# A linear-attention and MLP kernel on one core: the rows of a head's last part interleaved, one transfer for three, issued by ScalarE

## The chip, the cores and the metric

The kernel runs on one core of one Trainium2 chip. The metric is the device time in microseconds (us) of one execution. Three executions of the kernel before took 394.83, 394.56 and 392.82 us: a median of 394.56 us.

## What is computed

```
r, k, v, w: [4, 8, 768, 48] (batch, heads, sequence, head_dim), u: [8, 48]
state = 0                                  # [B, H, 48, 48]
for t in range(768):
    kt, vt, rt, wt = k[:, :, t], v[:, :, t], r[:, :, t], w[:, :, t]
    y[:, :, t] = rt @ (state + outer(u * kt, vt))
    state = wt[..., None] * state + outer(kt, vt)
x = y.transpose(0, 2, 1, 3).reshape(3072, 384)      # 8 heads of 48 side by side
h = max(x @ w1, x @ w2, x @ w3)                     # [3072, 768]
out = h @ w_out                                     # [3072, 384]
```

All arrays are float32.

## The kernel before, in words

The sequence is cut into chunks of 128 tokens. A unit is one chunk of one batch: 24 units (`NK`), numbered chunk by chunk. For each unit attention scales r and k by running products of the decay (VectorE scans, L397 and L412, and the product L421), makes scores on TensorE, masks them, and adds the part that comes from the carried state. ScalarE also squares the products to check that none ran out of range (L426). The result of a unit lies in a PSUM tile `y`, turned: feature by token.

Four units make one half (`HT` = 512 tokens), so there are six halves. `x` is a buffer of 128 partitions by 4 slots by 512 tokens, with two buffers in turn. ScalarE copies a unit's result from `y` to its columns of `x` (`result`, L627). Eight heads of 48 features must fill three slots of 128 rows. Each slot has one head in rows 0 to 47 and another in rows 64 to 111, which leaves rows 48 to 63 and 112 to 127 free. The two heads left over come in the fourth slot (`x[..., KT, ...]`, rows 0 to 47 and 64 to 111). Their 48 rows are spread, 16 each, over the free rows of slots 0 to 2. This is done by transfers within the on-chip memory, at L635: for each of the two heads three transfers of 16 rows, one per slot. In the first half only its last 256 columns need that; there VectorE's and ScalarE's work is densest, and the three transfers of the second head are on ScalarE's queue. In the other five halves all six are on SyncE's (SP's) queue, which also carries the loads of `tin` (L262), `kr` (L249), `v` (L252), the weights (L320) and the stores of the output (L755).

The MLP then works on `x` with products in two parts: ScalarE rounds a slot to `x_hi` (L134), VectorE makes the rest `x_lo` (L135), and TensorE multiplies both with the weights (`up`, L169), groups of nine matmuls of 512 columns; the second layer is `down`, L203. Weight rows are permuted on the host to match the rows of `x` (`row` in `_layout`).

The order of instructions on each engine is written out by hand: a string of steps (`PARTS`) for the first part, a round of steps (`ORD`) for each later unit, and a generator for the MLP. TensorE alternates between a half's MLP and later units of attention, and its order is fixed. Around a half's end the steps are: result of its fourth unit (L627), transfers (L635), the rest of the MLP of the half before, `x_hi` and `x_lo`, and the first `up` of the new half.

The kernel also has a slow path (after L807), taken if the check fails; it isn't taken here.

Of the kernel before, what the change touches and what calls it, by code (L numbers as in the profile page):

```python
# [39 lines left out]
ds = bass.ds  # L40

B, H, S, D = 4, 8, 768, 48
DM, FF = 384, 768
NP = 4
C = 128
# [9 lines left out]
HC = C // 2  # L55
VW = H * D * 3 // 2
NH = B * S // HT
KT = DM // 128
# [51 lines left out]
def kernel(ctx: ExitStack, tc, tin, nat, u_flat, u_pair, v_t, w_flat, out, ytr):  # L110
    nc = tc.nc
# [112 lines left out]
    with ExitStack() as fast:  # L224
# [391 lines left out]
        def result(k):  # L616

            half, slot = divmod(k, CPH)
            if half not in xt:
                xt[half] = x_p.tile([128, NP, HT], F32, name="x")  # L620
            x = xt[half]
            if k < SEW:
                nc.scalar.copy(out=x[:, 0:KT, slot * C:(slot + 1) * C], in_=prep[k]["y"])
                got.add(k)
                return
            to_x = x[0:112, :, slot * C:(slot + 1) * C].rearrange("p (h s) t -> p h s t", h=2)
            nc.scalar.copy(out=to_x, in_=prep[k]["y"][0:112])  # L627
            at, to = next(p for p in SUBS if p[0] <= slot < p[1]) if half == 0 else (0, CPH)
            got.add(k)
            due = all(half * CPH + i in got for i in range(at, to))  # L630
            cols = slice(at * C, to * C)
            for lo in (0, 64) if due else ():
                for j in range(KT):
                    eng = nc.scalar if lo and half == 0 else nc.sync
                    eng.dma_start(out=x[lo + 48:lo + 64, j, cols], in_=x[lo + 16 * j:lo + 16 * j + 16, KT, cols])  # L635

        steps = dict(m=midway, i=check_w, j=check_w, X=scores, M=take, T=transposes, R=from_state, U=to_state, S=state, Z=decayed, V=values, Y=values_more, E=result, n=load,
                     b=prep_scan_b, p=prep_floor, q=prep_inv, f=prep_scan_f, r=prep_rk, c=prep_check, d=prep_diag1, e=prep_diag2)
# [169 lines left out]
    with tc.If(rv != 0), ExitStack() as slow:  # L808
# [9 lines left out]
        with tc.For_i(0, B) as b:  # L818
            for pr in range(NP):
                wt = seq.tile([128, S], F32, name="wt")  # L820
                rt = seq.tile([128, S], F32, name="rt")
                kt = seq.tile([128, S], F32, name="kt")
                uk = seq.tile([128, S], F32, name="uk")
                uc = seq.tile([128, 1], F32, name="uc")
                vb = wk.tile([128, S], F32, name="vb")
                for t in (wt, rt, kt, uc):
                    nc.vector.memset(t[32:64, :], 0.0)
                for hh in range(2):
                    rows = slice(64 * hh, 64 * hh + 48)
                    for t, o in ((wt, pr * WS + 1), (rt, RK + pr * C), (kt, RK + (NP + pr) * C)):  # L830
                        for c in range(NCH):
                            nc.sync.dma_start(out=t[rows, c * C:(c + 1) * C],
                                              in_=tin[ds(b, 1), c, rows, o:o + C].rearrange("a p n -> (a p) n"))
                    nc.sync.dma_start(out=uc[rows, :], in_=u_pair[pr, hh])
                nc.vector.tensor_scalar(out=uk[0:112, :], in0=kt[0:112, :], scalar1=uc[0:112, :], scalar2=None, op0=ALU.mult)
                for j in range(KT):
                    with tc.For_i(0, 16) as i:
                        vb = wk.tile([128, S], F32, name="vb")
                        kv = wk.tile([128, S], F32, name="kv")
                        st = wk.tile([128, S + 1], F32, name="st")  # L840
                        yo = wk.tile([2, S], F32, name="yo")
                        nc.vector.memset(vb[32:64, :], 0.0)
                        for hh in range(2):
                            nc.sync.dma_start(
                                out=vb[64 * hh:64 * hh + 48, :],
                                in_=v_t[ds(b, 1), 2 * pr + hh, ds(i + 16 * j, 1), :].rearrange("a e t -> (a e) t").broadcast_to([48, S]))
                        nc.vector.memset(st[0:112, 0:1], 0.0)
                        nc.vector.tensor_tensor(out=kv[0:112, :], in0=kt[0:112, :], in1=vb[0:112, :], op=ALU.mult)
                        nc.vector.tensor_tensor_scan(out=st[0:112, 1:S + 1], data0=wt[0:112, :], data1=kv[0:112, :],
                                                     initial=0.0, op0=ALU.mult, op1=ALU.add)  # L850
                        nc.vector.tensor_tensor(out=kv[0:112, :], in0=uk[0:112, :], in1=vb[0:112, :], op=ALU.mult)
                        nc.vector.tensor_tensor(out=kv[0:112, :], in0=kv[0:112, :], in1=st[0:112, 0:S], op=ALU.add)
                        nc.vector.tensor_tensor(out=kv[0:112, :], in0=kv[0:112, :], in1=rt[0:112, :], op=ALU.mult)
                        for q in range(2):
                            z = ps_z.tile([2, S // 2], F32, name="z")
                            nc.tensor.matmul(z[:, :], lhsT=sel[0:112, :], rhs=kv[0:112, q * (S // 2):(q + 1) * (S // 2)],
                                             start=True, stop=True)
                            nc.vector.tensor_copy(out=yo[:, q * (S // 2):(q + 1) * (S // 2)], in_=z[:, :])
                        for hh in range(2):
                            slot, at = 2 * hh + pr // 2, 64 * (pr % 2)  # L860
                            if slot < KT:
                                dst = ytr[slot, ds(i + at + 16 * j, 1), ds(b, 1), :]
                            else:
                                dst = ytr[j, ds(i + at + 48, 1), ds(b, 1), :]
                            nc.sync.dma_start(out=dst.rearrange("a b t -> (a b) t"), in_=yo[hh:hh + 1, :])
# [54 lines left out]
def _layout(r, k, v, w, u, moe_w1, moe_w2, moe_w3, moe_w_out):  # L920

    def heads(a):
        return a.reshape(B, NP, 2, NCH, C, D).transpose(0, 3, 2, 5, 1, 4)

    tin = np.zeros((B, NCH, 128, TU), np.float32)
    tin[:, :, 48:64, :WC] = 1.0
    tin[:, :, :, :WC:WS] = 0.0
    for half in range(2):
        rows = tin[:, :, 64 * half:64 * half + D]
        rows[..., :NP * WS].reshape(B, NCH, D, NP, WS)[..., 1:] = heads(w)[:, :, half]  # L930
        rows[..., RK:RK + NP * C] = heads(r)[:, :, half].reshape(B, NCH, D, NP * C)
        rows[..., RK + NP * C:TU] = heads(k)[:, :, half].reshape(B, NCH, D, NP * C)
        rows[..., WC:WC + NP] = u.reshape(NP, 2, D)[:, half].T

    def natural(a):
        return a.reshape(B, H, NCH, C, D).transpose(0, 2, 3, 1, 4).reshape(B, NCH, C, H * D)

    nv, turned = natural(v), lambda a: np.roll(a[..., H * D // 2:], HC, axis=2)
    parts = [nv, turned(nv)]
    for a in (natural(k), natural(r)):  # L940
        a = np.concatenate([a[..., 0:H * D // 2], turned(a)], axis=3)
        parts.append(a.reshape(B, NCH, C, NP, 2, D).swapaxes(3, 4).reshape(B, NCH, C, H * D))
    nat = np.concatenate(parts, axis=3)
    padded = np.zeros((B, C, H, HC), np.float32)
    padded[..., 0:D] = nv[:, 0].reshape(B, C, H, D)
    late = np.roll(padded[:, :, NP:], HC, axis=1)
    bits = np.zeros((B, C, 2, KT, HC), np.float32)
    bits[..., D:HC] = late[:, :, 1::2, 0:D].reshape(B, C, 2, KT, D // KT)
    first = [padded[:, :, 0:NP].reshape(B, C, NP * HC), nv[:, 0, :, NP * D:], late[:, :, 0::2].reshape(B, C, 2 * HC), bits.reshape(B, C, DM)]
    nat[0:SEW, 0, :, 0:VW + DM] = np.concatenate(first, axis=2)[0:SEW]  # L950
    row = np.empty((KT, 128), np.int64)
    head = lambda j, par: 4 * (j % 2) + 2 * par + j // 2
    for j in range(KT):
        for par in range(2):
            row[j, 64 * par:64 * par + 48] = head(j, par) * D + np.arange(48)
            row[j, 64 * par + 48:64 * par + 64] = head(KT, par) * D + 16 * j + np.arange(16)
    ws = np.stack([moe_w1, moe_w2, moe_w3])
    w_in = ws[:, row.reshape(-1), :].reshape(3, KT, 128, FT, 128).transpose(3, 0, 2, 1, 4).reshape(3 * FT, 128, PC)
    w_all = np.concatenate([w_in, moe_w_out.reshape(FT, 128, DM)])
    if w_all.dtype == np.float64:  # L960
        w_all = np.append(w_all.reshape(-1), np.zeros(1)).view(np.int64)
    return {
        "tin": tin, "nat": nat, "u_flat": u.reshape(NP, 2, D).swapaxes(0, 1).reshape(H * D), "u_pair": u.reshape(NP, 2, D, 1),
        "v_t": v.transpose(0, 1, 3, 2), "w_all": w_all,
    }
# [18 lines left out]
```

## Time and profile before

| | |
|---|---|
| median of three executions | 394.56 us |
| the profiled execution | 396.12 us |
| its span | 394.4 us |
| TensorE busy | 384.3 us (97%) |
| VectorE, ScalarE, GpSimd busy | 261.1, 174.4, 79.3 us |
| bytes moved | 58.44 MB, a mean of 148 GB/s |
| transfers of L635 | 33 issued by SP, 3 by ScalarE |

The span is what the profiler recorded; the 1.7 us between it and the execution's own time lie outside. TensorE's busy time comes from modelled ends of pipelined matmuls: neighbours overlap, so that a short delay of a matmul can show as busy time. Starts of instructions tell more than the sum of busy times.

### The profile page before, as it was taken

To read this page: it belongs to the slowest core of one execution; us is meant where nothing else is said; L and a number is where in the kernel's file an instruction comes from. 1 tells how busy PE (TensorE), PEld (TensorE's weight loads), DVE (VectorE), ACT (ScalarE), POOL (GpSimd) and SP (SyncE) were. 2 spreads that over 40 slices of the span, in tenths; PEclk is the share of its full clock that TensorE was granted. 3 is DMA by queue.
4 is the path that set the end of the run, shared out by engine and by line. 5 is a ranking of instruction groups with operands and counts; after the bars stand their busy time and mean duration, and the time that the engine had idled before them with its cause. 6 is when DMAs were issued, how large, how long until landed. Compare 5 with 4: busy or idle time off the path is not lost.

```text
span 394.4 us, 10610 instructions
## 1 busy us (share of the span) xinstructions
PE 384.3 (97%) x4496; PEld 319.6 (81%) x4496; DVE 261.1 (66%) x399; ACT 174.4 (44%) x378; POOL 79.3 (20%) x102
## 2 busy tenths in 40 slices
PE   8999999999999999999999999999999999999994
PEld 3678876777688889888889888889888889878893
DVE  6899899987679976485688485688476531243310
ACT  4687788644434454334433533433543333331210
POOL 3000000131343252143134143134223100000000
PEclk9999999999999999999999999999999999999999
DMA  8992796403713431474342774342962113300011
GB/s 285 403 336 88 262 401 235 149 2 112 224 27 143 152 125 42 130 301 152 121 165 67 244 281 147 127 165 68 293 208 77 42 42 99 122 1 1 2 41 47
DMA packets 24680, 58.44 MB, mean 148 GB/s; under 512 B 3184, under 2 KB 6736, under 8 KB 24624
## 3 DMA queue, kind: packets, MB, share of 16 engines
q1 hardware_dynamic: 21216, 48.59, 35.6%
q10 hardware_dynamic: 3408, 9.09, 7.4%
q8 instruction: 37, 0.61, 0.7%
q14 instruction: 19, 0.16, 0.1%
HBM read 51.87 MB, written 4.72 MB: 143 GB/s over the span
## 4 chain that ended last, share of the span: by engine, by line
PE 86%; DMA 6%; DVE 3%; ACT 2%; issue 1%; SPq 1%; ACTq 0%
PE psm L169 54%; PE psm L203 16%; PE grams L480 3%; PE y L605 3%; PE y L518 3%; PE psm L502 2%; DMA x<-in_nat_dram 2%; DMA tin<-in_tin_dram 1%; DMA u_bc<-in_u_flat_dram 1%; PE grams L533 1%; DMA w<-in_w_all_dram 1%; DMA x<-x 1%; PE grams L203 1%; PE y L203 1%; PE grams L451 1%
## 5 line engine op out<-in xcount | busy, mean ns | idle before, releaser
L169 PE MATMUL psm<-x_hi,w 128*128 128x512 f32 x576 | 184.3, 394 | 0.2 <-ACT x_hi L134 0.2
L169 PEld LDWEIGHTS psm<-x_hi,w 128*128 128x128 f32 x576 | 108.2, 188 | 23.6 <-ACT x_hi L134 0.5
L169 PE MATMUL psm<-x_lo,w 128*128 128x512 f32 x288 | 112.5, 391 | 0.2 <-DVE x_lo L135 0.2
L154 DVE TENSOR_TENSOR m<-psm,m 128x512 f32<-128x512 f32 x64 | 43.8, 687 | 45.6 <-PE psm L169 42.9
L203 PE MATMUL psm<-w,h_hi 128*128 128x384 f32 x264 | 70.1, 362 | 0.0
L169 PEld LDWEIGHTS psm<-x_lo,w 128*128 128x128 f32 x288 | 54.1, 188 | 11.6 <-DVE x_lo L135 0.7
L203 PEld LDWEIGHTS psm<-w,h_hi 128*128 128x128 f32 x264 | 47.7, 188 | 5.0
L134 ACT CAST h_hi<-m 128x512 fp32r<-128x512 f32 x32 | 19.7, 620 | 44.0 <-DVE m L154 44.0
L203 PE MATMUL psm<-w,h_lo 128*128 128x384 f32 x116 | 38.9, 335 | 0.0
L461 POOL TENSOR_SCALAR_AFFINE_SELECT a<-sums 64x512 f32<-64x512 f32 x32 | 22.5, 703 | 72.2 <-DVE sums L458 71.1
L397 DVE TENSOR_TENSOR_SCAN gf<-tin,d_bwd 112x517 f32<-112x517 f32 x24 | 30.2, 1259 | 10.2 <-DMA tin<-in_tin_dram 9.0
L406 POOL TENSOR_SCALAR d_fwd<-gf 112x4 f32<-112x4 f32 x24 | 6.6, 277 | 142.3 <-DVE gf L397 134.7
L135 DVE TENSOR_TENSOR h_lo<-m,h_hi 128x512 fp32r<-128x512 f32 x32 | 23.7, 745 | 17.0 <-ACT h_hi L134 16.9
L169 PE MATMUL psm<-x,w 128*128 128x256 f32 (+1 forms) x126 | 33.9, 418 | 0.0
L412 DVE TENSOR_TENSOR_SCAN gf<-tin,d_fwd 112x517 f32<-112x517 f32 x24 | 33.1, 1380 | 0.3
L426 ACT ACTIVATE gf<-gf 112x1034 f32<-112x1034 f32 x24 | 25.7, 1070 | 10.3 <-DVE tin L421 10.2
L421 DVE TENSOR_TENSOR tin<-tin,gf 112x1024 f32<-112x1024 f32 x24 | 30.1, 1254 | 0.0
L438 POOL TENSOR_TENSOR kr<-kr,u_bc 128x384 f32<-128x384 f32 x16 | 28.6, 1790 | 1.3
L169 PEld LDWEIGHTS psm<-x,w 128*128 128x128 f32 x126 | 23.0, 190 | 6.7 <-issue 3.6
L135 DVE TENSOR_TENSOR x_lo<-x,x_hi 128x512 fp32r<-128x512 f32 x18 | 11.4, 689 | 21.9 <-ACT x_hi L134 14.2
L207 ACT COPY m<-psm 128x384 f32<-128x384 f32 x22 | 10.5, 476 | 30.4 <-PE psm L203 30.3
L152 ACT COPY m<-psm 128x512 f32<-128x512 f32 x32 | 18.5, 581 | 9.0 <-PE psm L169 7.7
(93 smaller groups left out, 462.8 us busy)
## 6 DMA issues: line engine op xcount, KB each, us to landing
tin<-in_tin_dram SPq DMA_DIRECT2D x24, 512.0 KB, 4.5
w<-in_w_all_dram SPq DMA_DIRECT2D x25, 384.0 KB, 7.5
w<-in_w_all_dram ACTq DMA_DIRECT2D x23, 384.0 KB, 3.6
v<-in_nat_dram SPq DMA_DIRECT2D x24, 288.0 KB, 5.3
tin<-in_tin_dram SPq DMA_DIRECT2D x24, 262.5 KB, 5.2
kr<-in_nat_dram SPq DMA_DIRECT2D x16, 384.0 KB, 5.1
out_dram<-m SPq DMA_DIRECT2D x22, 192.0 KB, 2.4
x<-x SPq DMA_DIRECT2D x30, 32.0 KB, 3.0
```

Of the source, the lines that this page charges most:

```text
L134: nc.scalar.copy(out=hi, in_=src)
L135: rest = lambda: nc.vector.tensor_tensor(out=lo, in0=src, in1=hi.bitcast(F32), op=ALU.subtract)
L152: nc.scalar.copy(out=m[:, cols], in_=ps[:, cols])
L154: nc.vector.tensor_tensor(out=m[:, cols], in0=ps[:, cols], in1=m[:, cols], op=ALU.max)
L169: nc.tensor.matmul(ps[:, cols], lhsT=wt[i][:, ct * 128:(ct + 1) * 128], rhs=x[part][:, ct, cols], start=(n == 0), stop=(n == KT * len(term ...
L203: nc.tensor.matmul(pss[tt][:, 0:DM], lhsT=ht[f][:, tok], rhs=wt[FT * 3 + f][:, :], start=(f == 0 and i == 0), stop=(f == FT - 1 and i == l ...
L397: nc.vector.tensor_tensor_scan(out=g[0:112, ::-1], data0=t[0:112, 0:WC][:, ::-1], data1=d_bwd[0:112, ::-1], initial=0.0, op0=ALU.mult, op1 ...
L412: nc.vector.tensor_tensor_scan(out=prep[k]["f"][0:112, :], data0=tbuf[k % NB][0:112, 0:WC], data1=d_fwd[0:112, :], initial=0.0, op0=ALU.mu ...
L421: nc.vector.tensor_tensor(out=both[0:112], in0=both[0:112], in1=by[0:112], op=ALU.mult)
L426: nc.scalar.activation(out=flat, in_=flat, func=AF.Square, accum_out=acc[0:112, k:k + 1])
L438: nc.gpsimd.tensor_tensor(out=n[:, 0, :], in0=n[:, 0, :], in1=u_bc[:, :], op=ALU.mult)
L461: nc.gpsimd.affine_select(out=a[o:o + HC, 0:H, :], in_=cs[o:o + HC, :].unsqueeze(2).broadcast_to([HC, H, HC]), pattern=[[0, H], [1, HC]], ...
```

## The change

In the first free rows of slot j stood rows 16j to 16j + 15 of the left-over head. After the change row n of the head goes to slot n mod 3: free row p of slot j takes row 3p + j. In this form one transfer from 48 partitions to 16 partitions by 3 slots says what three said. Two transfers per half stand where six stood: in the first half one on SP and one on ScalarE, in the other five both on ScalarE. The layout of the first chunk's values, the permutation of the weight rows and the slow path follow the new order of rows.

```
             due = all(half * CPH + i in got for i in range(at, to))
             cols = slice(at * C, to * C)
             for lo in (0, 64) if due else ():
-                for j in range(KT):
-                    eng = nc.scalar if lo and half == 0 else nc.sync
-                    eng.dma_start(out=x[lo + 48:lo + 64, j, cols], in_=x[lo + 16 * j:lo + 16 * j + 16, KT, cols])
+                eng = nc.scalar if lo or half else nc.sync
+                eng.dma_start(out=x[lo + 48:lo + 64, 0:KT, cols], in_=x[lo:lo + 48, KT, cols])
...
-                                in_=v_t[ds(b, 1), 2 * pr + hh, ds(i + 16 * j, 1), :].rearrange("a e t -> (a e) t").broadcast_to([48, S]))
+                                in_=v_t[ds(b, 1), 2 * pr + hh, ds(i * KT + j, 1), :].rearrange("a e t -> (a e) t").broadcast_to([48, S]))
...
-                                dst = ytr[slot, ds(i + at + 16 * j, 1), ds(b, 1), :]
+                                dst = ytr[slot, ds(i * KT + (at + j), 1), ds(b, 1), :]
...
-    bits[..., D:HC] = late[:, :, 1::2, 0:D].reshape(B, C, 2, KT, D // KT)
+    bits[..., D:HC] = late[:, :, 1::2, 0:D].reshape(B, C, 2, D // KT, KT).swapaxes(3, 4)
...
-            row[j, 64 * par + 48:64 * par + 64] = head(KT, par) * D + 16 * j + np.arange(16)
+            row[j, 64 * par + 48:64 * par + 64] = head(KT, par) * D + j + KT * np.arange(16)
```

On ScalarE, at the end of the second half (`gf` is the decay products, `m` an output tile, `w` a weight), the order before and the order of the change:

```order
L627 COPY x<-y 112x4x128
L426 ACTIVATE gf,sums<-gf 112x1034
L207 COPY m<-psm 128x384
L134 CAST w_1436<-w_217 128x768
L400 COPY dec_144<-gf 112x4
L134 CAST x_hi<-x 128x512 x3
```

```order
L627 COPY x<-y 112x4x128
L634 DMA x<-x 16x3x512 x2
L426 ACTIVATE gf,sums<-gf 112x1034
L207 COPY m<-psm 128x384
L134 CAST w_1428<-w_217 128x768
L400 COPY dec_144<-gf 112x4
L134 CAST x_hi<-x 128x512 x3
```

Two issues now stand between the result's copy and the check; nothing else changed place. At the ends of the third to sixth halves ScalarE has the same pair at the same place.

On SP, the same stretch before and after:

```order
L262 DMA tin_108<-in_tin_dram 128x525
L262 DMA tin_108<-in_tin_dram 128x1024
L635 DMA x<-x 16x512 x6
L249 DMA kr<-in_nat_dram 128x768
L252 DMA v<-in_nat_dram 128x576
L755 DMA out_dram<-m 128x384 x2
```

```order
L262 DMA tin_108<-in_tin_dram 128x525
L262 DMA tin_108<-in_tin_dram 128x1024
L249 DMA kr<-in_nat_dram 128x768
L252 DMA v<-in_nat_dram 128x576
L754 DMA out_dram<-m 128x384 x2
```

The six issues are gone from between the load of `tin` and that of `kr`.

## Rows read from the trace of the kernel before

**Rows 1.** The page, busy time of each engine.

```profile
PE 384.3 (97%) x4496; PEld 319.6 (81%) x4496; DVE 261.1 (66%) x399; ACT 174.4 (44%) x378; POOL 79.3 (20%) x102
```

**Rows 2.** Waits of TensorE: waiter, releaser, us in total, times, longest.

```profile
PE grams L451 <- DVE scur L554: 0.7, 1, 0.7
...
PE psm L169 <- DVE x_lo L135: 0.2, 1, 0.2
PE psm L169 <- ACT x_hi L134: 0.2, 1, 0.2
```

**Rows 3.** Timeline, 92 to 108 us: start, duration, engine, line [idle before <- releaser].

```profile
93.72 2.58 SPq L262 DMA_DIRECT2D tin<-in_tin_dram  x2
...
94.80 0.58 ACT L627 COPY x<-y 112x512 f32<-112x512 f32 x1 [0.58 <-PE y L605]
...
96.39 4.68 SPq L635 DMA_DIRECT2D x<-x  x6
...
102.07 1.66 ACT L134 CAST x_hi<-x 128x512 fp32r<-128x512 f32 x3 [1.83 <-DMA x<-x]
...
102.72 1.90 DVE L135 TENSOR_TENSOR x_lo<-x,x_hi 128x512 fp32r<-128x512 f32 x3 [3.51 <-ACT x_hi L134]
```

**Rows 4.** The same timeline, TensorE alone.

```profile
102.19 0.34 PE L203 MATMUL psm<-w,h_lo 128*128 128x384 f32 x1
...
102.75 0.50 PE L169 MATMUL psm<-x_hi,w 128*128 128x512 f32 x1 [0.22 <-ACT x_hi L134]
...
103.47 0.50 PE L169 MATMUL psm<-x_lo,w 128*128 128x512 f32 x1 [0.23 <-DVE x_lo L135]
...
103.81 0.63 PE L169 MATMUL psm<-x_hi,w 128*128 128x512 f32 x2
```

**Rows 5.** TensorE's timeline at the start of the fourth half, 210 to 226 us.

```profile
222.36 0.33 PE L203 MATMUL psm<-w,h_lo 128*128 128x384 f32 x1
...
222.99 0.62 PE L169 MATMUL psm<-x_hi,w 128*128 128x512 f32 x2
```

**Rows 6.** Line L635: issue durations in ns min/median/max; landing in us min/median/max.

```profile
L635 SPq DMA_DIRECT2D x<-x x33: 512/585/1592, 38.7 to 334.7; - x33
...
L635 ACTq DMA_DIRECT2D x<-x x3: 602/612/856, 38.7 to 40.3; - x3
...
DMA to landing us min/median/max: 1.8/2.3/4.5
```

**Rows 7.** Timelines of ACT, SP and DVE, 36 to 76 us, one after another.

```profile
38.73 2.15 ACTq L635 DMA_DIRECT2D x<-x  x3
40.93 1.28 ACT L434 ACTIVATE kr<-tin 112x128 f32<-112x128 f32 x4 [2.23 <-issue]
...
38.73 1.87 SPq L635 DMA_DIRECT2D x<-x  x3
...
43.29 1.23 DVE L397 TENSOR_TENSOR_SCAN gf<-tin,d_bwd 112x517 f32<-112x517 f32 x1 [1.14 <-ACT gf L426]
```

**Rows 8.** Timelines of ACT, DVE and PE, later in that stretch.

```profile
54.30 0.37 ACT L152 COPY h_hi<-psm 128x256 f32<-128x256 f32 x1
...
54.88 0.42 DVE L154 TENSOR_TENSOR h_hi<-psm,h_hi 128x256 f32<-128x256 f32 x1
...
74.05 0.70 PE L451 MATMUL grams<-tin,kr 48*64 48x64 f32 x32 [0.69 <-DVE scur L554]
```

**Rows 9.** Timelines of ACT and PE at the start of the fifth half.

```profile
279.30 1.66 ACT L134 CAST x_hi<-x 128x512 fp32r<-128x512 f32 x3 [0.50 <-DMA x<-x]
...
280.97 0.39 PE L169 MATMUL psm<-x_hi,w 128*128 128x512 f32 x1
```

**Rows 10.** Busy time of each engine by stretch: us, PE, PEld, DVE, ACT, POOL, clock, DMA share, GB/s.

```profile
50.00:60.00 10.00, 10.00 (x109) 6.64 (x110) 9.86 (x16) 8.33 (x18) 0.22 (x1) 1.00 1.03 401
95.38:102.07 6.69, 6.69 (x27) 4.66 (x26) 1.88 (x3) 2.37 (x6) 1.32 (x2) 1.00 0.49 143
...
273.81:279.30 5.49, 5.49 (x34) 5.49 (x33) 2.53 (x4) 2.98 (x9) 1.37 (x3) 1.00 0.52 144
```

## The prediction

> **What bounds the kernel now.** I read the page first. TensorE is busy for 384.3 us of the 394.4 us span [rows 1]; its order is fixed and the change removes no matmul, so only waits of TensorE can be won. I then listed those waits. Most belong to the start of the program. Three can touch this change: 0.2 us for `x_hi` and 0.2 us for `x_lo` before L169, once each, and one of 0.7 us for VectorE's new state (L554) before L451 [rows 2]. The reader sees from this list alone that the prize is about 1 us in 394, and that there is nothing to win at the other ends of halves: `x_hi` and `x_lo` each made TensorE wait once, although six halves begin.
>
> Those times use modelled ends of matmuls, so I went to the starts in the timeline. At the start of the second half TensorE begins its last L203 at 102.19, and the third matmul on the new `x` begins at 103.81, which is 1.62 us later [rows 4]. At the start of the fourth half, where nothing is waited for, the same sequence takes 222.36 to 222.99, or 0.63 us [rows 5]. The late `x` costs 1.62 - 0.63 = 0.99 us there. Upstream the reader sees why. ScalarE has the result in `x` at 95.38 (94.80 + 0.58). SP is still busy with a load of `tin` from 93.72 and starts the first transfer at 96.39; six issues take 4.68 us, to 101.07; `x_hi` starts at 102.07 after ScalarE sat idle for 1.83 us for the transfer; and VectorE's `x_lo` at 102.72 [rows 3]. Most of the 6.7 us from result to `x_hi` is spent issuing.
>
> **Term 1: the second half.** The change takes away six issues on SP and puts two on ScalarE, right behind the copy. Three issues on ScalarE's queue have a median of 612 ns, and 33 on SP one of 585 ns [rows 6]. What an issue with three rows per destination row costs isn't in the trace. Its bounds are 0.51 us, the shortest issue of one part, and 1.84 us, three of ScalarE's (3 x 0.612). I take 0.61 us, since it is one instruction of the same kind with the same 16 destination rows. Two end at 95.4 + 1.2 = 96.6. Landing takes 1.8 to 4.5 us after an issue [rows 6]; because the load of `tin` is in flight then, I take the 4.5: 101.1. One `x_hi` cast is 0.62 us later and one `x_lo` 0.69 us after that (1.66 us for three casts, 1.90 us for three differences with their overlaps [rows 3]), so the first pair is there at about 101.7 and 102.4. TensorE without a delay wants them at 102.36 and 102.59 (a step of about 0.17 us after 102.19 and one of about 0.23 us, as 0.63 us makes three steps [rows 5]). The wait goes: -0.99 us. With the bounds of issue and landing, `x` is complete between 95.4 + 1.0 + 1.8 = 98.2 and 95.4 + 3.7 + 4.5 = 103.6. The late end is 1.5 us past today's 102.07, so this term lies between -0.99 and +1.5 us.
>
> The Trainium skill speaks against the step to another queue ("DMA: Bandwidth & Descriptors", section "Issuing engines are not separate DMA queues"): transfers from several engines share the same DMA engines, and only the sequencer's time to issue is saved, "which is usually small relative to the DMA itself". By that rule term 1 would be near 0, and the time 394.1. The trace differs at this place: six issues take 4.68 us and a landing 2.3 us in the median.
>
> **Term 2: the first half.** At 38.73 ScalarE issues three transfers in 2.15 us, and then starts L434 at 40.93 with 2.23 us of waiting put down to issuing; SP spends 1.87 us on its three. Further down ScalarE's queue VectorE waits 1.14 us for ScalarE's check (L426) before its scan at 43.29 [rows 7]. One issue in place of three frees ScalarE about 1.4 us earlier (2.15 - 0.61 = 1.5 at most), so this wait of 1.14 us goes. VectorE then shows no idle time until it releases L554, for which TensorE waits 0.69 us at 74.05 [rows 8]. How much of the 1.14 us is still there 30 us later depends on what VectorE would wait for next. The tightest place that I found is L154 at 54.88, behind ScalarE's copy that ends at 54.67 (54.30 + 0.37) [rows 8]: 0.21 us of room. That copy stands behind work that waits for weights, and SP's two issues fewer let the next weight loads go about 1.3 us earlier (1.87 - 0.6), so the room may be wider. The DMA engines are full here (share 1.03, 401 GB/s [rows 10]), and a start that much earlier shortens the backlog. The gain lies between 0 and 0.69 us; I take the middle of 0.21 and 0.69: -0.45 us.
>
> **What costs nothing.** In the second to sixth halves ScalarE gets 1.2 us of issuing behind the copy. The transfers wait for the copy's end, and behind them stand the check, an output copy (L207) and `dec`. ScalarE is busy for 2.37 of 6.69 us between copy and `x_hi` in the second half and 2.98 of 5.49 us in the fifth [rows 10], so idle times of 4.3 and 2.5 us cover it. Without that cover it would cost up to 1.2 us at an end of a half. An earlier `x` in the later halves earns nothing, since `x_hi` already starts before TensorE asks: at 279.30 for 280.97 [rows 9]. SP's 33 issues become 1, and loads of `kr` and `v` and the stores go out up to 4.7 us earlier; TensorE shows no wait for them, so 0. The permuted rows, the layout and the slow path move the same bytes: 0.
>
> **The sum** is -0.99 - 0.45 = -1.44 us. Against the profiled execution's own 396.12 us that gives 394.7, and against the median of 394.56, which I use, 393.1 us. I count 0.5% (2.0 us) as the least that a measurement can tell from no change; the three executions themselves lie 2.0 us apart.
>
> **The rivals.**
> 1. *The issues were not the delay.* `x` still lands at about 102, because the transfers wait behind the `tin` load in the DMA engines. For it: landings of up to 4.5 us [rows 6]. Against it: the first transfer would start 1 us sooner on a queue of its own, and the last issue ended only at 101.07 [rows 3]. This is also what the skill's rule above would make of it. Then only term 2 is left: 394.56 - 0.45 = 394.1 us.
> 2. *More than I count.* Term 2 comes in full (-0.69 us), and ScalarE's and VectorE's earlier start shortens some of the small delays that modelled ends hide, by 0.3 us or more: 394.56 - 0.99 - 0.69 - 0.3 = 392.6 us or less. For it: VectorE is busy for 9.86 of 10 us at 50 to 60 us [rows 10], so any time it wins may count. Against it: no row shows those hidden delays.
> 3. *ScalarE pays.* A merged issue costs three single ones, 1.84 us, or 3.7 us for a pair. In the fifth half 2.5 us of idle time cover it and 1.2 us are left; `x_hi` starts 1.67 us before TensorE needs it [rows 9], of which a cast and a difference take about 1.3 less a step of 0.23, so some 0.6 us is lost. The second half would keep at least part of its gain. From 393.1 + 0.6 to 393.1 + 1.6, with 394.2 in the middle.
> 4. *The merged transfer does not spread* over the DMA engines, and so the time gets worse. An engine moves about 401 / 16 = 25 GB/s [rows 10]; one transfer has 48 x 512 x 4 bytes = 98 KB, 3.9 us on one engine, and two in line 7.9 us. With 0.6 us of issue and 2.3 us of landing `x` is complete 10.8 us after the copy: 106.2 in the second half, with `x_hi` at 106.8, 4.4 us too late in place of 0.99. In the fifth half, whose copy ends at 273.81 (where its stretch of rows 10 begins), it is complete at 284.6, 5.3 us after today's 279.30; with 1.67 - 0.62 = 1.05 us of cover that is 4.3 us late; the fourth and sixth are alike. Together 3.4 + 3 x 4.3 - 0.45 = 15.9, or 410 us. It decides from the point where the pair lands more than about 7 us after the copy. Against it: 16 destination rows are what each single transfer had, and those landed in 2.3 us; the 48 source rows are the new thing.
>
> By the skill's rule on how many engines a transfer uses (same page, section "Why a DMA increments its semaphore by 16 and not by 1"), the largest number up to 16 that divides the outer sizes of both sides counts; 16 divides 48 and 16, so rival 4 falls. No row shows how the transfers were split.
>
> **How the numbers follow.** My forecast has a chance of 0.50, rival 1 0.14, rival 2 0.24 (with the draws of the forecast that a spread of 2 us puts beyond 0.5%), rival 3 0.08, rival 4 0.04. Faster by over 0.5% is rival 2: 0.24. Slower is rival 4: 0.04. The rest is within 0.5%: 0.72. The likeliest is 393.1 us. The range goes down past rival 2 by the 1 us that the executions lie to one side, 391.6, and up past rivals 1 and 3 to 395.2, which also holds part of term 1's bad end; rival 4 and the tails are left out.
>
> **What would show it.** Right: in the second half the transfers start at the copy's end on ScalarE's queue, about 1 us before today's place; `x_hi` waits for no transfer; third matmul on the new `x` 0.63 us after the last L203; no wait of VectorE for L426 near 42 us, and a wait of under 0.5 us before L451 near 74. Later halves show the same starts relative to their copy. Wrong: landings of the pair over 5 us, issues over 1 us, a new wait of TensorE at the start of a half, or a time that moves by over 2 us while these waits do what I say.

## The result and the profile after

The change takes 396.14 us in the median of 20 executions (393.71 to 399.97), the kernel before, timed beside it, 393.85 us (392.02 to 395.31): ratio 1.0057, 95% interval 1.0038 to 1.0076. It is slower, by 2.3 us, just over what the prediction called measurable; the forecast was 1.44 us faster, and 396.14 lies above the range. The profiled execution of the change took 399.25 us (span 397.3), that of before 396.12 (span 394.4). Both are long executions, 3.1 and 2.3 us above their medians: they show how time is lost, and the medians how much.

The page first: busy times and the granted clock of TensorE in 40 slices.

```profile
PE 385.8 (97%) x4496; PEld 320.5 (81%) x4496; DVE 259.7 (65%) x399; ACT 174.2 (44%) x378; POOL 77.5 (20%) x102
...
PEclk9999999999899999999999999999999999999999
```

TensorE is busy for 1.5 us more than in [rows 1] with the same 4496 matmuls, and one slice of its clock (99 to 109 us) reads 8. So matmuls ran slower somewhere there; that alone is not a wait. Its waits are next, in the form of [rows 2].

```profile
PE psm L169 <- ACT x_hi L134: 1.7, 1, 1.7
...
PE psm L169 <- DVE x_lo L135: 0.7, 2, 0.5
...
PE grams L451 <- DVE scur L554: 0.2, 1, 0.2
```

The wait for L554 fell from 0.7 to 0.2: the first half did what term 2 said. The two waits for `x`, which were to vanish, grew from 0.2 and 0.2 to 1.7 and 0.7. The timeline of the second half's start, to be held against [rows 3]:

```profile
93.19 1.94 SPq L262 DMA_DIRECT2D tin<-in_tin_dram  x2
...
94.26 0.58 ACT L627 COPY x<-y 112x512 f32<-112x512 f32 x1 [0.59 <-PE y L605]
...
94.88 1.25 ACTq L634 DMA_DIRECT2D x<-x  x2
...
95.17 0.42 SPq L249 DMA_DIRECT2D kr<-in_nat_dram  x1
...
95.65 0.58 SPq L252 DMA_DIRECT2D v<-in_nat_dram  x1
...
102.63 0.99 POOL L437 TENSOR_TENSOR kr<-kr 128x384 f32<-128x384 f32 x1 [5.63 <-DMA kr<-in_nat_dram]
102.96 1.66 ACT L134 CAST x_hi<-x 128x512 fp32r<-128x512 f32 x3 [3.27 <-DMA x<-x]
103.61 2.71 DVE L135 TENSOR_TENSOR x_lo<-x,x_hi 128x512 fp32r<-128x512 f32 x3 [4.96 <-ACT x_hi L134]
...
103.63 0.50 PE L169 MATMUL psm<-x_hi,w 128*128 128x512 f32 x1 [1.66 <-ACT x_hi L134]
...
105.77 0.80 PE L169 MATMUL psm<-x_lo,w 128*128 128x512 f32 x1 [0.45 <-DVE x_lo L135]
```

Up to the issue all goes as predicted: ScalarE has the result at 94.84 (94.26 + 0.58), and both transfers are issued by 96.13, where SP needed until 101.07. But `x_hi` starts 8.12 us after the result (102.96 - 94.84), before it was 6.69 (102.07 - 95.38). The loads of `kr` and `v`, which stood behind six issues on SP, leave SP at 95.17 and 95.65, so `kr` is issued ahead of the second transfer, which starts at 95.52, and `v` behind its start. The same stretch by DMA issues (KB each, median us from issue to landing), before:

```profile
kr<-in_nat_dram SPq DMA_DIRECT2D x1, 384.0 KB, 3.5
v<-in_nat_dram SPq DMA_DIRECT2D x1, 288.0 KB, 3.7
...
x<-x SPq DMA_DIRECT2D x6, 32.0 KB, 3.9
```

And after:

```profile
tin<-in_tin_dram SPq DMA_DIRECT2D x1, 512.0 KB, 6.0
...
kr<-in_nat_dram SPq DMA_DIRECT2D x1, 384.0 KB, 7.3
v<-in_nat_dram SPq DMA_DIRECT2D x1, 288.0 KB, 8.5
...
x<-x ACTq DMA_DIRECT2D x2, 96.0 KB, 6.6
```

An `x` transfer now lands after 6.6 us in the median (7.4 the later, as line L634 shows below, so 5.8 the other), `kr` after 7.3 in place of 3.5, `v` after 8.5 in place of 3.7. Issuing was cheap, as counted; line L634 over the whole program:

```profile
L634 ACTq DMA_DIRECT2D x<-x x11: 563/603/672, 38.7 to 335.3; - x11
...
DMA to landing us min/median/max: 2.3/2.9/7.4
```

What the late `x` cost in this execution can be read off. From TensorE's last L203 to the third matmul on the new `x`, 0.63 us where nothing is late [rows 5], it took 1.62 us before [rows 4] and 3.05 after (101.64 to 104.69): 1.43 us more. The next matmul on an `x_lo` then waits as well; from the third, it starts 1.08 us on, before 0.47: 0.61 us more. And then each step takes twice its time. Windows of 1 us (busy time of PE, PEld, DVE, ACT, POOL; clock, DMA share, GB/s):

```profile
100.00:101.00 1.00, 1.00 (x5) 0.61 (x4) 0.00 (x0) 0.00 (x0) 0.00 (x0) 1.00 1.11 215
...
102.00:103.00 1.00, 0.00 (x0) 0.00 (x0) 0.00 (x0) 0.04 (x1) 0.37 (x1) 1.00 0.53 180
...
104.00:105.00 1.00, 0.78 (x4) 0.49 (x3) 1.00 (x2) 0.99 (x3) 1.00 (x1) 1.00 0.00 2
105.00:106.00 1.00, 0.55 (x3) 0.23 (x2) 1.00 (x2) 0.00 (x0) 0.72 (x2) 0.75 0.12 45
106.00:107.00 1.00, 1.00 (x3) 0.81 (x4) 1.00 (x3) 0.00 (x0) 0.00 (x0) 0.50 1.14 232
107.00:108.00 1.00, 1.00 (x3) 0.79 (x3) 1.00 (x3) 0.46 (x1) 0.00 (x0) 0.50 0.82 266
...
109.00:110.00 1.00, 1.00 (x6) 0.83 (x5) 0.20 (x1) 0.00 (x0) 0.00 (x0) 1.00 0.72 277
```

The granted clock is 1.00 through the wait, 0.50 (1.2 GHz) from 106 to 108 and 1.00 again from 109. Seven matmuls took 3.15 us (105.77 to 108.92) where seven at full clock take 1.59: 1.56 us. Together 1.43 + 0.61 + 1.56 = 3.60 us. Landmarks of TensorE, taken from the chain of waits that ended last, give the same: from the first half's first L169 to the run of 33 matmuls behind L451 it took 50.71 us before and 50.22 after (-0.49); from there to the first L518 behind the second half's start 41.41 and 45.01 (+3.60); from there to the last run of L169 235.26 and 235.16.

### The profile page after: what moved, and what is told of

The parts are those of the page before. It is cut to its first block, busy times and chain, and to the rows that moved or that the text cites. A ratio compares the mean times of both kernels' runs of the same rounds, so it can differ in the third digit from the quotient of the medians.

```text
span 397.3 us, 10559 instructions
## 1 busy us (share of the span) xinstructions
PE 385.8 (97%) x4496; PEld 320.5 (81%) x4496; DVE 259.7 (65%) x399; ACT 174.2 (44%) x378; POOL 77.5 (20%) x102
## 4 chain that ended last, share of the span: by engine, by line
PE 85%; DVE 6%; DMA 5%; issue 1%; ACT 1%; SPq 0%; ACTq 0%; DVEq 0%
PE psm L169 54%; PE psm L203 16%; PE grams L480 3%; PE y L605 3%; PE y L518 3%; DMA x<-x 2%; PE psm L502 2%; DMA x<-in_nat_dram 2%; DMA tin<-in_tin_dram 1%; PE grams L533 1%; DVE cv L343 1%; DVE w L349 1%; DVE x_lo L135 1%; PE grams L203 1%; PE y L203 1%
## 5 line engine op out<-in xcount | busy, mean ns | idle before, releaser
L169 PE MATMUL psm<-x_hi,w 128*128 128x512 f32 x576 | 185.1, 396 | 1.7 <-ACT x_hi L134 1.7
L169 PEld LDWEIGHTS psm<-x_hi,w 128*128 128x128 f32 x576 | 108.8, 189 | 25.3 <-ACT x_hi L134 2.0
L169 PE MATMUL psm<-x_lo,w 128*128 128x512 f32 x288 | 113.2, 393 | 0.7 <-DVE x_lo L135 0.7
L203 PE MATMUL psm<-w,h_hi 128*128 128x384 f32 x264 | 70.0, 361 | 0.0
L169 PEld LDWEIGHTS psm<-x_lo,w 128*128 128x128 f32 x288 | 54.5, 189 | 12.4 <-DVE x_lo L135 1.4
L203 PEld LDWEIGHTS psm<-w,h_hi 128*128 128x128 f32 x264 | 47.7, 188 | 5.0
L203 PE MATMUL psm<-w,h_lo 128*128 128x384 f32 x116 | 38.9, 335 | 0.0
L169 PE MATMUL psm<-x,w 128*128 128x256 f32 (+1 forms) x126 | 33.9, 418 | 0.0
L412 DVE TENSOR_TENSOR_SCAN gf<-tin,d_fwd 112x517 f32<-112x517 f32 x24 | 32.1, 1338 | 0.3
L426 ACT ACTIVATE gf<-gf 112x1034 f32<-112x1034 f32 x24 | 25.6, 1070 | 11.5 <-DVE tin L421 10.0
L169 PEld LDWEIGHTS psm<-x,w 128*128 128x128 f32 x126 | 23.0, 190 | 6.8 <-issue 3.8
L438 POOL TENSOR_TENSOR kr<-kr,u_bc 128x384 f32<-128x384 f32 x16 | 27.4, 1716 | 1.3
L135 DVE TENSOR_TENSOR x_lo<-x,x_hi 128x512 fp32r<-128x512 f32 x18 | 12.2, 732 | 19.5 <-ACT x_hi L134 19.5
```

The lines of the kernel that those rows point to most:

```text
L135: rest = lambda: nc.vector.tensor_tensor(out=lo, in0=src, in1=hi.bitcast(F32), op=ALU.subtract)
L169: nc.tensor.matmul(ps[:, cols], lhsT=wt[i][:, ct * 128:(ct + 1) * 128], rhs=x[part][:, ct, cols], start=(n == 0), stop=(n == KT * len(term ...
L203: nc.tensor.matmul(pss[tt][:, 0:DM], lhsT=ht[f][:, tok], rhs=wt[FT * 3 + f][:, :], start=(f == 0 and i == 0), stop=(f == FT - 1 and i == l ...
L412: nc.vector.tensor_tensor_scan(out=prep[k]["f"][0:112, :], data0=tbuf[k % NB][0:112, 0:WC], data1=d_fwd[0:112, :], initial=0.0, op0=ALU.mu ...
L426: nc.scalar.activation(out=flat, in_=flat, func=AF.Square, accum_out=acc[0:112, k:k + 1])
L438: nc.gpsimd.tensor_tensor(out=n[:, 0, :], in0=n[:, 0, :], in1=u_bc[:, :], op=ALU.mult)
```

## The experiments

Two theories were set against each other. (The expectations name others beside them: what ScalarE's issuing costs, and the `tin` load alone.) **Collision**: taken off SP, the six issues no longer hold back `kr` and `v`, whose 672 KB now share the DMA engines with the pair and with `tin`. **Form**: the merged rows, or ScalarE's queue, make the transfers slow in themselves. Three measures stand in the table for each profile: from the end of ScalarE's copy (L627) to `x_hi`; the delay at the third matmul on the new `x` over the 0.63 us; and the middle, from the first L169 of the first half (as the chain of waits has it, 0.16 us behind the timeline) to the end of VectorE's last copy, which leaves out the program's start and end.

| kernel (profiles in the order taken) | copy to `x_hi` | delay at third matmul | middle |
|---|---|---|---|
| before | 6.69, 6.11 | 0.99, 0.43 | 365.21, 364.27 |
| the change | 8.12, 7.55 | 2.42, 1.88 | 368.22, 367.73 |
| pair on SP | 5.73, 6.07, 6.39 | 0.05, 0.39, 0.72 | 364.31, 364.66, 365.02 |
| change, `kr` and `v` held | 5.98, 6.49 | 0.30, 0.81 | 363.94, 364.43 |
| pair on SP, held | 6.01 | 0.33 | 363.99 |
| six on ScalarE | 7.79 | 2.10 | 368.45 |
| before, `kr` and `v` ahead | 9.27 | 3.57 | 367.70 |
| first half alone merged | 6.63 | 0.94 | 364.61 |

**The merged pair on SP's queue**, with two further profiles. Against the change:

```
-                eng = nc.scalar if lo or half else nc.sync
+                eng = nc.scalar if lo and half == 0 else nc.sync
```

> The merged pair of the second to sixth halves goes back to SP's queue, between the loads of tin and kr; the first half stays as in the change. Theory A (collision): the pair lands late in the second half because SP no longer stands in the way of the loads of kr and v, which then share the DMA engines with it. In SP's order the pair is ahead of kr and v again, so it lands 3 to 4.5 us after its issue near 96.4, x_hi waits little and TensorE not at all: about 392.4 us (before 393.85, less 0.5 for the first half and 1.0 for the second). Theory B (form): three rows per destination row move slowly beside other traffic, whatever the queue: landing of 6 to 7 us again, a wait of over 1 us before L169 and 395.5 to 396.5 us. Theory C (ScalarE's issuing costs): like A in time, about 393.

> The kernel of the merged pair on SP once more, for a second profile: its times were of two kinds, two executions near 392.4 and ten near 395.4 us, and the profile was of a fast one. If this execution is of the slow kind: theory A says that the pair lands later than the 5.1 us seen, beside kr and v, and TensorE waits over 1 us before L169 in the second half; if the delay is elsewhere (first half, later halves), the second half's start will look as in the first profile.

> Third look at the pair of merged transfers on SP's queue, whose earlier profiles were short while its median was long. If the pair on SP lands late in some executions: a profile with landings over 5.5 us, an x_hi wait of TensorE over 0.5 us and a granted clock under 0.8 between 104 and 109 us. If the length comes from the end alone (the last output store): pair landing 4.6 to 5.1 us again, no x_hi wait, the same 364 to 365 us from the first x matmul to VectorE's last copy.

Measured: 395.39 us (12 executions), ratio 1.0028 (1.0007 to 1.0048); the two further profiled executions took 394.28 and 396.06. Theory A's 392.4 us did not come; the median is next to theory B's 395.5. The landings are theory A's. In all three profiles the pair, now issued ahead of `kr` and `v`, landed in 4.6 to 5.2 us, and TensorE waited for no `x_hi`. So merged rows are not slow in themselves, and loads that are issued behind the pair hardly hold it up. What stayed is a delay some matmuls later, in the first profile's timeline:

```profile
100.97 2.72 DVE L135 TENSOR_TENSOR x_lo<-x,x_hi 128x512 fp32r<-128x512 f32 x3 [3.16 <-ACT x_hi L134]
...
102.08 1.07 POOL L437 TENSOR_TENSOR kr<-kr 128x384 f32<-128x384 f32 x1 [5.34 <-ACT x_hi L134]
...
103.22 1.34 POOL L438 TENSOR_TENSOR kr<-kr,u_bc 128x384 f32<-128x384 f32 x1
...
103.75 0.50 PE L169 MATMUL psm<-x_lo,w 128*128 128x512 f32 x1 [0.37 <-DVE x_lo L135]
```

`kr` is there early, so GpSimd's L437 and L438 run beside VectorE's three `x_lo`, which take 2.72 us in place of 1.90 [rows 3], and the third `x_lo` is 0.4 us late. The Trainium skill has this ("GPSIMD Engine Reference", section "Specifications"): GpSimd contends with VectorE instructions that have two SBUF inputs. The traces agree: in the six profiles with L437 or L438 beside the `x_lo` the three take 2.71 us or more, in the eight others 1.89 or 1.90. In the change it is L438, from 103.70, and the `x_lo` that begins beside it takes 1.50 us in place of 0.69. No run moved GpSimd's work alone. This delay does not make the median: it is longer than two of the three profiled executions (392.81 and 394.28 us). The third has a middle of 365.02 and its length mostly from the program's start and end. What makes the other executions long stays open.

**The change with `kr` and `v` of that unit held** until one output store is issued, timed in two sessions (`N` loads one unit's `kr` and `v`):

```
-           n10 w f9 o V7 X8 Z9 Y7 U8 E7 m8 e8 D1 l c8 D5 s b10 d9 p10 x l S8 D6 o M8 D2 G12 r9 s t G13 G2 G0 t G14 G1 e9 o
+           n10 w f9 o V7 X8 Z9 Y7 U8 E7 m8 e8 D1 l c8 D5 s b10 N9 d9 p10 x l S8 D6 o M8 D2 G12 r9 s t G13 G2 G0 t G14 G1 e9 o
...
-            if k + 1 < NK:
+            if k + 1 < NK and k != CS:
...
-        steps = dict(m=midway, i=check_w, j=check_w, X=scores, M=take, T=transposes, R=from_state, U=to_state, S=state, Z=decayed, V=values, Y=values_more, E=result, n=load,
+        steps = dict(N=load_nat, m=midway, i=check_w, j=check_w, X=scores, M=take, T=transposes, R=from_state, U=to_state, S=state, Z=decayed, V=values, Y=values_more, E=result, n=load,
```

> The change with one thing moved: the loads of kr and v for the tenth unit are issued after one store of the output, so at about 99.3 us instead of 95.2; the pair stays on ScalarE's queue. Theory A (collision with kr and v): the pair shares the DMA engines with the tin load alone, lands in 3 to 4.5 us, by 100, no wait of TensorE at the second half's start, about 392.4 us. Theory B (form) and a theory that the tin load alone is what delays it: landing of 5.8 to 7.4 us as in the change, and 395.5 to 396.5 us. Theory C (ScalarE's issuing costs): no gain over the change, about 396.

> The change with the loads of kr and v of the next unit held back until one output store is issued, timed again in more rounds. Collision theory: the pair lands by 99.5 to 100 us, TensorE waits for no x at the second half, the granted clock stays at 1.00 there; 392.5 to 393.3 us median, 0.6 to 1.3 below the kernel before. Rival (the first gain was the chip's spread): 393.6 to 394.2 us, ratio 1.000.

Measured: 392.83 us, ratio 0.9976 (0.9956 to 0.9996), and then 394.11 us, ratio 1.0013 (0.9999 to 1.0028). The timeline of the first:

```profile
94.51 1.22 ACTq L634 DMA_DIRECT2D x<-x  x2
...
98.92 1.47 SPq L249 DMA_DIRECT2D kr<-in_nat_dram  x1
...
100.46 1.66 ACT L134 CAST x_hi<-x 128x512 fp32r<-128x512 f32 x3 [1.13 <-DMA x<-x]
...
101.11 1.90 DVE L135 TENSOR_TENSOR x_lo<-x,x_hi 128x512 fp32r<-128x512 f32 x3 [2.57 <-ACT x_hi L134]
...
101.44 0.40 PE L169 MATMUL psm<-x_hi,w 128*128 128x512 f32 x1
...
101.86 0.50 PE L169 MATMUL psm<-x_lo,w 128*128 128x512 f32 x1
```

The collision is confirmed twice: with the same merged form and the same queue, `x_hi` starts 5.98 and 6.49 us after the copy in place of 8.12 and 7.55, the wait for `x_hi` is gone, and the clock stays at 1.00. Set against before, though, the gain of the first session did not come again: the second time is the rival's (393.6 to 394.2 us). The second profile shows why there is so little of it. The pair was issued by 95.13 and still landed after 6.0 us in the median, the later one at 100.3 and not by 100:

```profile
tin<-in_tin_dram SPq DMA_DIRECT2D x1, 512.0 KB, 7.0
x<-x ACTq DMA_DIRECT2D x2, 96.0 KB, 6.0
```

The last load of `tin` was issued at 92.70 and landed 7.0 us later, at 99.7; `x_hi` started at 100.36. In the profiles of before (two), of this kernel (two) and of the next one, `x_hi` starts 0.3 to 1.5 us after that load of `tin` has landed, whether the last `x` issue ends at 95.1 or at 101.1. That is what rival 1 says. It is argued from these times: no run moved the load of `tin`. Nor is the order strict: in the first profile with the loads held, the earlier transfer of the pair landed after 3.2 us, at 97.7, when `tin` landed at 100.1.

**Both: pair on SP, loads held.** The edits of the two experiments above together.

> Merged pair on SP's queue as in the first experiment, and the loads of kr and v for the tenth unit held behind one store as in the second. Theory A: the queue does not matter, what else is in flight does; 392.8 us like the second experiment, no second kind of times near 395.4. If ScalarE's queue of its own is what helped the second experiment: 394 to 395.4 us.

Measured: 394.09 us, ratio 0.9992 (0.9968 to 1.0016), level with before and not the 392.8 expected. `x_hi` 6.01 us after the copy, delay 0.33 us, `x_lo` 1.89 us: the same as on ScalarE's queue. Which queue issues the pair does not matter once the loads are held. Against the pair on SP without holding (1.0028) only the held loads differ, so the loads cost time there too, though they are issued behind the pair; of that the three profiles show only the slower `x_lo`. No version beats the kernel before by more than a measurement can tell; these two, with the loads held, are level with it.

**Six single transfers, ScalarE's queue.** Against the kernel before:

```
-                    eng = nc.scalar if lo and half == 0 else nc.sync
+                    eng = nc.scalar if lo or half else nc.sync
```

> The kernel before with its six single transfers of the later halves moved to ScalarE's queue; no merging and the old order of rows. Theory A: SP is free as in the change and loads kr and v at 95.2, so the singles land late as well: x_hi waits until 103 or later, 396 us or more (six issues of 0.6 us end near 98.5, later than the pair's). Theory B (form): singles land in 2 to 4.5 us, x_hi near 101, and the time is that of before less up to 0.5: 393.3 to 393.9 us.

Measured: 398.51 us, ratio 1.0112 (1.0084 to 1.0140). Nothing is merged, and `x` is late all the same: `kr` leaves SP at 95.80, the six land in 5.3 us in the median, `x_hi` starts 7.79 us after the copy, and the clock is 0.72 in the mean of 104 to 110. Here ScalarE's queue does cost: its check (L426) starts only at 100.01, behind 4.63 us of issuing.

**Before, with `kr` and `v` ahead of the six on SP.** Nothing merged, no change of queue; against the kernel before:

```
-           n10 w f9 o V7 X8 Z9 Y7 U8 E7 m8 e8 D1 l c8 D5 s b10 d9 p10 x l S8 D6 o M8 D2 G12 r9 s t G13 G2 G0 t G14 G1 e9 o
+           n10 w f9 o V7 X8 Z9 Y7 U8 N9 E7 m8 e8 D1 l c8 D5 s b10 d9 p10 x l S8 D6 o M8 D2 G12 r9 s t G13 G2 G0 t G14 G1 e9 o
```

with the same two lines on `load_nat` as above.

> The kernel before with the loads of kr and v of the tenth unit issued ahead of the second half's six transfers on SP's queue; nothing is merged and the queue stays SP's. Collision theory: the six land later than the 4.5 us of before, x_hi starts at 104 us or later (two issues of SP alone, 0.8 us, would put it at 102.9), TensorE waits over 1 us for x_hi, the granted clock falls below 0.8 after it, 395.5 to 397.5 us. Rival (the loss lies in the merged form or in ScalarE's queue): the six land in 4.5 us, no clock fall, 393.9 to 394.7 us.

Measured: 396.75 us, ratio 1.0067 (1.0039 to 1.0096), as slow as the change; the six landed in 5.6 us in the median. Its timeline:

```profile
95.57 0.42 SPq L249 DMA_DIRECT2D kr<-in_nat_dram  x1
96.04 0.42 SPq L252 DMA_DIRECT2D v<-in_nat_dram  x1
96.56 3.67 SPq L635 DMA_DIRECT2D x<-x  x6
...
103.81 1.66 ACT L134 CAST x_hi<-x 128x512 fp32r<-128x512 f32 x3 [4.41 <-DMA x<-x]
...
104.47 0.51 PE L169 MATMUL psm<-x_hi,w 128*128 128x512 f32 x1 [2.80 <-ACT x_hi L134]
```

The order of the issues alone makes a loss of the same size: `x_hi` comes 2.6 to 3.2 us later than in the two profiles of before (9.27 against 6.69 and 6.11). Of that 1.0 us is the issuing of the two loads on SP, which the change does not have; the rest is landing. `x_hi` started just short of the 104 us expected. One expectation failed outright. TensorE waits 2.8 us, longer than in the change, and yet in this execution the clock stays at 1.00:

```profile
102.00:103.00 1.00, 0.00 (x0) 0.00 (x0) 0.00 (x0) 0.00 (x0) 0.23 (x2) 1.00 0.09 18
...
104.00:105.00 1.00, 0.51 (x1) 0.19 (x1) 0.55 (x1) 1.00 (x3) 0.00 (x0) 1.00 0.00 0
...
106.00:107.00 1.00, 1.00 (x6) 0.82 (x5) 1.00 (x3) 0.00 (x0) 0.00 (x0) 1.00 0.30 106
...
108.00:109.00 1.00, 1.00 (x6) 0.81 (x6) 1.00 (x2) 0.90 (x2) 0.00 (x0) 1.00 0.82 243
```

**The first half alone merged**, the later halves as six single transfers on SP:

```
+                if half == 0:
+                    eng = nc.scalar if lo else nc.sync
+                    eng.dma_start(out=x[lo + 48:lo + 64, 0:KT, cols], in_=x[lo:lo + 48, KT, cols])
+                    continue
...
+                    nc.sync.dma_start(out=x[lo + 48:lo + 64, j, cols], in_=x[lo + j:lo + 48:KT, KT, cols])
```

> Only the first half has merged transfers (one on SP, one on ScalarE); the later halves have six single ones on SP at their old place, each from every third row. This prices the first half alone. By the change's trace it wins 0.5 us: the wait of TensorE for L554 near 74 falls from 0.69 to 0.2 us, and the second half starts 0.5 us earlier. Expected 393.3 us against 393.85 of before, with the second half's start as late against the result as before (about 1 us lost). If the gain at 74 is eaten later: 393.85.

Measured: 393.89 us, ratio 0.9998 (0.9981 to 1.0014). In the trace the stretch up to the 33 matmuls behind L451 takes 50.23 us, 0.48 less than in the first profile of before, and the wait for L554 is 0.2. So term 2 is in the trace, but the median is the 393.85 of "eaten later" and not 393.3: no time shows it.

**Filler matmuls against the clock's fall.** The change with `W8` (eight matmuls on a constant, results unused) put into the table of steps between `D2` and `G12`, so that they stand between the last L203 and the first matmul on the new `x`.

> The change with eight bf16 matmuls of 512 columns on zeros (results unused) in front of the second half's first matmul, so that TensorE works while x is late. They take about 1.75 us, as much as the wait of 1.66 us that the change's trace shows. Theory D (the fall of the granted clock to 0.50 after the wait costs as much as the wait): no fall, the 1.5 us of slow matmuls after 105.8 go, 394.5 us. Rival (the clock costs nothing, x_lo is late anyway): 396.1 us or somewhat more, since in executions where x comes early the eight matmuls themselves cost up to 1.75 us.

Measured: 396.06 us, ratio 1.0042 (1.0012 to 1.0073). That is the rival's time, but the run is inconclusive on the clock: in the profiled execution `x` landed earlier (3.5 and 5.6 us), so the fillers, 1.9 us long, delayed TensorE themselves, and the three `x_lo` took 3.52 us. No fall of the clock was there to be prevented. The profile shows something else:

```profile
94.44 1.23 ACTq L634 DMA_DIRECT2D x<-x  x2
...
95.58 0.42 SPq L249 DMA_DIRECT2D kr<-in_nat_dram  x1
```

Here SP was busy with `tin` until 95.52, so `kr` left after the issue of the second transfer had begun (95.1). In both profiles of the change `kr` left before it (95.17 before 95.5, 94.52 before 95.0), and there the pair landed in 5.8 to 7.4 us. In the change the two queues race, and which order comes out differs from execution to execution. That may be part of why its times spread from 393.7 to 400.0; no run counts it.

**A second profile of both kernels.** The change, unedited:

> The changed kernel once more, for a second profile. Its 20 times spread from 393.7 to 400.0 us. Theory A: the spread is the landing of the pair in the second half (5.8 to 7.4 us in the first profile), with the wait before L169 and the clock after it; everything from the third half on is the same within 0.2 us.

Measured: 396.07 us. The pair landed in 6.3 us in the median, TensorE waited 1.1 us for `x_hi` and 0.7 for `x_lo`, the clock was 0.50 from 105 to 107. The same picture with a shorter wait, but not the theory: this execution is 3.18 us shorter than the first, and the middles differ by 0.49 (368.22 and 367.73). The rest lies in the program's start and end. From the third half on the two are alike, as expected. The kernel before, unedited:

> The kernel before, looked at a second time: nothing is edited. Its first profile took 396.1 us, over 2 us above its median. Collision theory: x of the second half lands in 4 to 5 us again, x_hi starts behind the same chain, TensorE waits 0.2 to 0.4 us for x there and the time from the first x matmul to VectorE's last copy is 365.2 to 365.6 us, so that 393 to 394 us in all come from a shorter start and end. Rival (the kernel before is as fast as the held loads in most executions): x lands in under 4 us, the middle is 364.0 to 364.6 us.

Measured: 394.31 us. Here the rival's numbers came, not the theory's:

```profile
95.76 4.65 SPq L635 DMA_DIRECT2D x<-x  x6
...
100.95 1.66 ACT L134 CAST x_hi<-x 128x512 fp32r<-128x512 f32 x3 [1.27 <-DMA x<-x]
...
102.35 0.50 PE L169 MATMUL psm<-x_lo,w 128*128 128x512 f32 x1 [0.16 <-DVE x_lo L135]
```

`x` landed in 3.5 us (3.9 in the first profile), the delay at the third matmul was 0.43 us and the middle 364.27, not 365.2 to 365.6. What the prediction took for the kernel's delay, 0.99 us, was that of one execution on the late side.

## Why the prediction was wrong

- **The step that failed** stands in "what costs nothing": "loads of `kr` and `v` and the stores go out up to 4.7 us earlier; TensorE shows no wait for them, so 0". The first half of the sentence is what happened: `kr` is issued 0.3 us after the copy, where it was 5.7 (95.17 - 94.84 and 101.12 - 95.38). The zero asked only whether somebody waits for these loads, not whom they hold up. They came to share the DMA engines with the pair, `kr` ahead of its second transfer, and that is priced by two experiments from both sides: held back, the change loses its wait and is within measurement of before (0.9976 and 1.0013); put ahead of the six in the kernel before, they make it as slow as the change (1.0067).
- **Term 1** (-0.99 us) came out as +3.60 between the first profiles of both kernels, and as +3.1 to +4.2 over the two profiles of each. The issue term was right: 603 ns each, 0.61 taken. The landing was mis-sized: 4.5 us taken as its late end, 5.8 and 7.4 measured, so `x` was complete at 102.9, not 101.1. With -0.49 for the first half the two profiled executions are explained (3.11 of 3.13 us); the medians lie 2.3 us apart. That it could be late at all stood in the prediction's own bound of +1.5 us; the first step, 1.43 us, is inside that. The other 2.17 us, a slower `x_lo` (0.61) and the clock (1.56), had no term.
- The prize itself was too large, and its reading was wrong. "Most of the 6.7 us from result to `x_hi` is spent issuing" does not hold: `x_hi` of the first slot waits for the fourth of the six transfers, which brings the second head's rows of that slot. Line L635, that transfer alone, before:

```profile
L635 SPq DMA_DIRECT2D x<-x x1: 588/588/588, 98.2 to 98.2; - x1
...
  ACT x_hi L134: 1.8, 1
...
DMA to landing us min/median/max: 3.8/3.8/3.8
```

It was issued 2.8 us after the copy (98.2 - 95.38) and then took 3.8 us to land; `x_hi`, at 102.07, started before the sixth had landed (102.5). A merged pair brings all slots at once, so `x_hi` waits for its second transfer whole. With the loads held that one is issued 0.6 us after the copy and lands in 5.3 and 5.8 us: 2.2 us of earlier issuing are mostly spent again in landing. Three profiles with six single transfers on SP behind `tin` (before twice, the first half alone merged) lose 0.99, 0.43 and 0.94 us at this place, 0.79 in the mean; with the pair unhindered 0.30, 0.81 and 0.33 are still lost, 0.48 in the mean, with `x` landing about when `tin` does. So **rival 1**, with a chance of 0.14, had the right limit for the gain, though not for the time of the change: with the loads held, some 0.3 us of term 1 come. The Trainium skill's rule that was set against term 1 ("DMA: Bandwidth & Descriptors", section "Issuing engines are not separate DMA queues") is borne out in its first half and its consequence: transfers of two queues hold each other up (`kr` landed after 7.3 in place of 3.5 us), and the time saved on a sequencer (4.68 to 1.25 us) bought next to nothing. Its "usually small relative to the DMA itself" is not so here, where six issues took 4.68 us and their landing 3.9 in the median.
- **Term 2** (-0.45) fits the first profile of before (-0.49) and is twice what the second gives (-0.22); no time shows it.
- **Rivals 2 to 4** fell: nothing more was gained than counted; a merged issue costs no more than a single one; and merged pairs spread, with a median landing of 2.9 us over all halves against 2.3 of single ones. In the second half the pair was complete 8.0 us after the copy, past rival 4's 7, but the same merged form lands in 4.6 to 5.2 us there when it is issued ahead of the loads. Two of the prediction's signs of being wrong came as written: landings of the pair over 5 us and a longer wait of TensorE. No rival had the loads as the thing that comes late next, so the losing side of the forecast rested on the wrong mechanism.
- **The clock** is the part that is not settled. In the two profiles of the change and in that with six on ScalarE it fell after the wait, in that with the loads ahead it did not. An execution's mean granted clock says little of that, for it also counts the program's end: the change's profile reads 0.50 from 396 to 397 us, with TensorE at rest. At a mean of 1.000 neither can weigh much. Five executions of the change at 1.000 have spans of 391.8 to 393.9 us (392.5 in the mean), and 22 of before, in three other sessions, 389.8 to 392.9 (391.2). So the change seems about 1.3 us behind where the clock holds; the spans overlap, and this is rough. Three executions of the change at 0.994 have spans of 396.7 to 397.3 us. What decides whether the clock falls was not found, and the fillers did not tell.

## What to carry to other kernels

When an issue is taken off a queue, ask what stood behind it: those transfers start earlier, and if they use the DMA engines while something urgent is in flight, they must be priced as if they had been put in front of it. A queue full of issues can be doing the work of a priority; whoever removes it has to put the order back by hand, here by holding two loads behind a store. And take a delay of under 1 us that is to be won from two profiles of the same kernel before it is made a term.

## What was not expected of the hardware

- From 100 to 102 us the DMA share of the change reads 1.11 and 1.03 at only 215 and 223 GB/s, where SP's loads moved 401 GB/s at 1.03 [rows 10]. The engines were occupied at half the bytes. The transfers of `x` are not the whole reason: the queue with the loads accounts for 83% of the engines' time in those 2 us and the pair's for 20%, and from 106 to 107 us the share is 1.14 at 232 GB/s with no `x` transfer in flight. The cause stays open.
- After waits of 1.1, 1.3 and 1.7 us the granted clock fell to 0.50 (1.2 GHz) some 2 us after TensorE had started again, which cost 1.56 us more in the change's first profile; after a wait of 2.8 us, in one execution, it did not fall.
- The first x matmul starts between 22.85 and 24.16 us, and the span ends 3.4 to 5.7 us after VectorE's last copy starts, in kernels that are alike there. That is up to 3.6 us from places that the change doesn't touch, more than any term of the forecast.
